# Decay products in PSUM halves, a new rank for the first layer, and a result stored in pieces of 64 tokens

## The chip, the cores and the metric
The program runs on one core of one Trainium2 chip. The metric is the device time of one execution in microseconds (us). Before the change it is 2306.92 us, the median of 3 runs (2304.29 to 2314.39).

## The reference, cut to what matters
Three layers follow one another. `B, H, S, D` = 4, 8, 768, 40.

```python
# 1. a recurrence over 768 steps for each of 32 heads, state is 40 x 40
for t in range(S):
    y[t] = r[t] @ state
    Sa = state @ a[t]
    state = state * w[t][None, :] - outer(Sa, b[t]) + outer(v[t], k[t])
# x: 3072 tokens x 320
# 2. first layer, d_ff = 2048, weights given as 64-bit floats
h = x @ w_in;  x = (h * cos(h)) @ w_out
# 3. second layer: 8 experts, d_ff = 1024
P = exp(logits - max); 8 rounds of dividing by row sums and column sums
out = sum over e of P[:, e] * (relu(x @ w1[e]) @ w2[e])
```

## The kernel before, in words
**Stages.** The recurrence is cut into 24 chunks of 32 steps. The 32 heads lie as 16 pairs, so that most attention tiles have 80 partitions (two heads of 40) and 16 blocks of 32 columns. For each chunk n there are three functions. `early(n)` (line 664) loads decays, a, b, k, r and v, forms the running products of the decays from the front and from behind, scales a, b and k with them, multiplies them on TensorE, and inverts a 32 x 32 triangle per head: the triangle goes through a DRAM tile (`LD`) into another layout, 62 small GpSimd instructions do the inversion (`inverse`, line 707), and the result goes back through another DRAM tile (`UD`). `late(n)` (line 722) fetches that inverse and prepares transposed factors. `chain(n)` (line 764) carries the state from chunk n-1 to chunk n and writes the chunk's output y to a DRAM tile `XT`. Chunks form pairs: after every second chunk `moe1(i)` (line 939) runs the first layer on the pair's 256 tokens and writes `ZD`. Only when the recurrence is over does its memory come free for the second layer (`moe2`, line 1068), a long run of matmuls on all 3072 tokens: for each expert, six groups of 512 tokens. `combine` (line 1037) adds an expert's part to an accumulator of 128 tokens x 320, and at the last expert stores it.

**Decays.** In `early` the decay tile P has 16 blocks of 33 columns (a marker column, then 32 decays) and one column behind them. Two scans over all 529 columns, on VectorE, multiply along; a constant tile `d1` restarts the product at every marker. The scan from behind writes another SBUF tile, Q. Then Q is divided by the block's full product (`iPC`), a is multiplied by the products from the front (80 x 1024), and b and k by the divided ones, in two halves of 80 x 512. Two ScalarE squares with a running sum fill `flag` and `flagP`, from which a number range is judged at the end of the recurrence. P is triple buffered: the load of chunk n+3 waits until chunk n's chain has read it.

**Order of the work.** No queue order is written by hand. A recorder takes all operations, and `order` (line 353) places them with a list scheduler that has its own costs. At each point an engine takes, of what is ready, the operation with the smallest key. The key is a rank from `PRIORITY` (line 577, the first number), and within a rank the longer way still to go comes first, with an offset in microseconds (base + slope x group number) that can push a group forward. A rank without a base goes by the order of the program. Before: the chain, the decoding of the first layer's weights (`prep`) and the first layer (`one`) have rank 0; `early`, `late` and `y` have rank 1. Where TensorE would idle during the scheduler's first 800 us, it places filler matmuls of 64 x 64 on a constant.

**PSUM.** The 8 banks form three pools: A (4 banks: attention, decoding, logits, the second layer's first product), M and N (2 each: the first layer's sums and products, and the second layer's sums). `nc.bank("A", False)` takes a bank at its first use, and it comes free after the last use.

**Decoding.** The 64-bit weights of the first layer come in 32 pieces. Each is decoded by five VectorE and several ScalarE instructions through a bank of pool A, beside the first chunks.

**The store.** At the last expert each of 24 accumulators (128 partitions x 320) goes out with one DMA on the SP queue, whose target is a view of 2 batches x 64 tokens x 320.

Of the kernel before, what the change touches and what calls it, by code (L numbers as in the profile page):

```python
# [6 lines left out]
F32 = mybir.dt.float32  # L7
F32R = mybir.dt.float32r
I32 = mybir.dt.int32
ALU = mybir.AluOpType  # L10
AF = mybir.ActivationFunctionType
AX = mybir.AxisListType
# [60 lines left out]
def lay_out(x):  # L73
# [17 lines left out]
    w = np.zeros((NCH, FR, U * (C + 1) + 1), rows["w"].dtype)  # L91
    w[:, :, :-1].reshape(NCH, FR, U, C + 1)[..., 1:] = rows["w"]
    out["tw"] = w
    out["tabk"] = np.concatenate([apart(rows["a"]), flat(rows["b"]), flat(rows["k"])], 2)
# [454 lines left out]
def sinkhorn(nc, ident, P, sk, red, ones, bank):  # L549
# [27 lines left out]
PRIORITY = {  # L577
    "chain": (0, 0, 0), "y": (1, 0, 0), "early": (1, 0, 0), "late": (1, 0, 0), "prep": (0, None, 0),
    "one": (0, 0, 0), "gate": (2, 0, 0), "two": (3, None, 0), "fetch": (4, None, 0),
}  # L580
# [11 lines left out]
class Kernel:  # L592
    def __init__(self, sb, ps, dr, a):
# [8 lines left out]
        self.at2 = tile("at2", AT2_COLS, F32)  # L602
        self.flag = tile("flag", NCH + 2, F32)
        self.nc = nc = Recorder(ps, {"A": (4, 5, 6, 7), "M": (0, 1), "N": (2, 3)}, {x.name for x in a.values()})
# [19 lines left out]
    def attention_setup(self):  # L624
# [3 lines left out]
        self.P = [t2(U * 33 + 1) for _ in range(3)]  # L628
        self.Q = t(U * 33 + 1)
        self.invP = self.Q[:, 1:].rearrange("p (u s) -> p u s", u=U)[:, :, 1:33]  # L630
        self.ABK = [t(4 * U * 32) for _ in range(3)]
# [19 lines left out]
        self.iPC = t2(U)  # L651
        self.flagP = t2(NCH)
        self.LD = [self.dr.tile([U, 2, C, C], F32, name=f"LD{i}") for i in range(2)]
# [10 lines left out]
    def early(self, n):  # L664
# [6 lines left out]
        self.load(n)  # L671
        nc.vector.tensor_tensor_scan(self.Q[0:80, ::-1], P[0:80, ::-1], c["d1"][0:80, ::-1], 0.0, op0=ALU.mult, op1=ALU.max)
        nc.vector.tensor_tensor_scan(P[0:80], P[0:80], c["d1"][0:80], 0.0, op0=ALU.mult, op1=ALU.max)
        nc.vector.reciprocal(self.iPC[0:80], P3[0:80, :, 32])
        nc.vector.tensor_tensor(self.invP[0:80], self.invP[0:80], self.iPC[0:80].unsqueeze(2).to_broadcast([80, U, 32]), op=ALU.mult)
        A2 = Ax[0:80].rearrange("p u (h s) -> p u h s", h=2)
        nc.vector.tensor_tensor(A2, A2, P3[0:80, :, 0:32].unsqueeze(2).to_broadcast([80, U, 2, 32]), op=ALU.mult)
        ps = nc.bank("A")
        for q in range(2):
            u = slice(8 * q, 8 * q + 8)  # L680
            nc.vector.tensor_tensor(BK[0:80, :, u], BK[0:80, :, u],
                                    self.invP[0:80, u].unsqueeze(1).to_broadcast([80, 2, 8, 32]), op=ALU.mult)
            for i in range(8 * q, 8 * q + 8):
                k, o = divmod(i, 2)
                nc.tensor.matmul(ps[64 * o:64 * o + 64, 64 * k:64 * k + 64], lhsT=Ax[0:80, i, :], rhs=BK[0:80, :, i, :],
                                 start=True, stop=True)
        g = ps.rearrange("p (u s) -> p u s", u=8)
        nc.scalar.activation(Lb, g[:, :, 0:32], AF.Copy)
        nc.vector.tensor_tensor(Lkm, g[:, :, 32:64], c["lmask"].unsqueeze(1).to_broadcast([128, 8, 32]), op=ALU.mult)
        ps = nc.bank("A")  # L690
        for x, f in ((P3[0:80, :, 1:33], self.flagP), (self.invP[0:80], self.flag)):
            nc.scalar.activation(ps[0:80].rearrange("p (u s) -> p u s", u=U), x, AF.Square, accum_out=f[0:80, n:n + 1])
        LD, UD = self.LD[n % 2], self.UD[n % 2]
# [158 lines left out]
    def moe1_weights(self):  # L852
# [20 lines left out]
        for f in range(16):  # L873
# [5 lines left out]
                out=s[:, 0:768].bitcast(I32), in_=a["win"].bitcast(I32)[f])  # L879
            A, Bl = decode(nc, self.c["expo"], st, nc.bank("A", False)[:, 0:384], w[:, 384:768].bitcast(F32R), -1)  # L880
            hi = w[:, 0:384].bitcast(F32R)
# [6 lines left out]
            nc.sync.dma_start(out=s[:, 0:640].bitcast(I32), in_=a["moe_w_out"].bitcast(I32)[128 * f:128 * f + 128, :])  # L888
            A, Bl = decode(nc, self.c["expo"], st, nc.bank("A", False)[:, 0:320], w[:, 960:1280].bitcast(F32R), -1)
            hi, lo = w[:, 640:960].bitcast(F32R), w[:, 960:1280].bitcast(F32R)  # L890
# [146 lines left out]
    def combine(self, e, t, ps4):  # L1037
        nc = self.nc
        out = self.a["out"]
        for j in range(4):  # L1040
# [9 lines left out]
            if e == E - 1:  # L1050
                i, j2 = divmod(tt, 2)
                nc.sync.dma_start(out=out.rearrange("(b t) d -> b t d", b=B)[2 * j2:2 * j2 + 2, 64 * i:64 * i + 64, :], in_=acc)

    def in_range(self):

        nc, f = self.nc, self.flag
        nc.group = ("gate", 0)
        nc.vector.tensor_reduce(f[0:80, NCH:NCH + 1], self.flagP[0:80], axis=AX.X, op=ALU.add)

    def decide(self, out):  # L1060
        nc, f = self.nc, self.flag
        nc.group = ("gate", 0)
        nc.vector.tensor_reduce(f[0:80, NCH + 1:NCH + 2], f[0:80, 0:NCH + 1], axis=AX.X, op=ALU.add)
        ps = nc.bank("A")
        nc.tensor.matmul(ps[0:1, 0:1], lhsT=f[0:80, NCH + 1:NCH + 2], rhs=self.ones[0:80, 0:1], start=True, stop=True)
        nc.vector.tensor_scalar(out[0:1, 0:1], ps[0:1, 0:1], 1e16, None, op0=ALU.is_lt)
# [243 lines left out]
```

## Time and profile before

| what | us |
|---|---|
| median of 3 runs | 2306.92 |
| the profiled execution | 2302.23 |
| its span, first to last instruction | 2300.5 |
| TensorE busy, 18773 matmuls | 2258.6 (98%) |
| VectorE busy | 1058.9 (46%) |
| ScalarE busy | 820.1 (36%) |
| GpSimd busy | 658.8 (29%) |
| mean granted TensorE clock | 0.995 |

Busy times are unions over the span. TensorE's counts the filler matmuls as well, so a busy TensorE is no proof of useful work in the first 800 us. All operations carry one line number (L519, the place where the scheduler's list is emitted), so that groups are told apart by their tiles and shapes: `at` are attention's tiles, `r1a` and `r1b` the weights (later the accumulators), `r` and `fs` the layers' working tiles, `cst` constants, `ps` PSUM.

### The profile page before, as it was taken

What the parts mean: (1) busy time and instruction counts of PE and PEld (TensorE: products, weight loads), DVE (VectorE), ACT (ScalarE), POOL (GpSimd) and SP (SyncE); (2) the same over time, 40 slices, a digit from 0 to 9 for tenths busy, and PEclk for the clock granted to TensorE, in tenths of its full rate; (3) what the DMA queues carried; (4) which work ended last, traced back from release to release, by engine and by line L of the source; (5) the groups of instructions that cost most, each with busy time, mean ns of one, the idle gap of its engine ahead of it and who ended that gap; (6) DMA issues with size and microseconds to landing.
All of it is one profiled execution on the core that took longest, in us unless ns stands there. A gap on an engine that the chain in (4) does not pass through costs nothing.

```text
span 2300.5 us, 45714 instructions
## 1 busy us (share of the span) xinstructions
PE 2258.6 (98%) x18773; PEld 2064.7 (90%) x18773; DVE 1058.9 (46%) x2106; ACT 820.1 (36%) x1710; POOL 658.8 (29%) x1694
## 2 busy tenths in 40 slices
PE   8999999999999999999999999999999999999997
PEld 7889999999999997999999989999988999999886
DVE  8878877888878653411222222222222222222222
ACT  5456655565656564224112112113113113112111
POOL 2858486677864731002002002002002002001000
PEclk9999999999999999999999999999999999999999
DMA  8343433444433233001001001001001001000000
GB/s 227 95 111 89 103 92 70 101 103 106 103 89 92 63 95 98 1 1 51 1 1 51 1 1 51 1 1 51 1 1 51 1 1 51 1 1 7 24 23 25
DMA packets 155496, 116.85 MB, mean 51 GB/s; under 512 B 112528, under 2 KB 134032, under 8 KB 153360
## 3 DMA queue, kind: packets, MB, share of 16 engines
q1 hardware_dynamic: 155280, 113.86, 19.7%
q8 instruction: 149, 2.44, 0.4%
q14 instruction: 67, 0.55, 0.1%
HBM read 95.73 MB, written 18.09 MB: 49 GB/s over the span
## 4 chain that ended last, share of the span: by engine, by line


## 5 line engine op out<-in xcount | busy, mean ns | idle before, releaser
L519 DVE SCALAR_TENSOR_TENSOR r<-ps,r 128x512 fp32r<-128x512 f32 x384 | 265.5, 692 | 971.0 <-ACT r L519 971.0
L519 PE MATMUL ps<-r1a,r 128*128 128x320 f32 x4248 | 669.5, 310 | 0.4 <-DVE r L519 0.4
L519 ACT ACTIVATE r<-ps 128x512 fp32r<-128x512 f32 x480 | 286.4, 597 | 1042.2 <-PE ps L519 1023.9
L519 PEld LDWEIGHTS ps<-r1a,r 128*128 128x128 f32 x4248 | 637.0, 188 | 15.5 <-DVE r L519 0.7
L519 POOL TENSOR_TENSOR at<-at 128x60 f32<-128x60 f32 (+24 forms) x1488 | 518.1, 348 | 276.0 <-DMA at<-LD 160.2
L519 PE MATMUL ps<-at,r1a 128*128 128x512 f32 x2352 | 579.1, 397 | 0.0
L519 PEld LDWEIGHTS ps<-at,r1a 128*128 128x128 f32 x2352 | 435.9, 188 | 93.8
L519 PE MATMUL ps<-at 128*64 128x72 f32 (+6 forms) x6064 | 446.4, 248 | 11.8 <-DMA at<-UD 4.6
L519 PEld LDWEIGHTS ps<-at 80*64 80x64 f32 (+4 forms) x6064 | 385.1, 147 | 54.7 <-issue 8.2
L519 POOL TENSOR_TENSOR r1a<-at,r1a 128x256 fp32r<-128x256 f32 (+2 forms) x147 | 101.4, 693 | 804.2 <-ACT r1a L519 794.5
L519 PE MATMUL ps<-at,r 128*128 128x320 f32 (+1 forms) x1128 | 182.6, 314 | 0.0
L519 PEld LDWEIGHTS ps<-at,r 128*128 128x128 f32 (+1 forms) x1128 | 167.4, 184 | 9.3
L519 PE MATMUL ps<-cst 128*64 128x64 f32 x2400 | 162.3, 225 | 4.3 <-DMA cst<-in_consts 4.1
L519 PEld LDWEIGHTS ps<-cst 128*64 128x64 f32 x2400 | 149.9, 139 | 14.0 <-issue 5.8
L519 PE MATMUL ps<-r,r1a 128*128 128x256 f32 x960 | 138.8, 291 | 3.1 <-ACT r L519 2.1
L519 POOL TENSOR_TENSOR at<-at,at 128x256 fp32r<-128x256 f32 (+2 forms) x45 | 31.1, 692 | 355.3 <-ACT at L519 350.2
L519 ACT ACTIVATE at<-ps 80x320 f32<-80x320 f32 (+4 forms) x234 | 92.7, 417 | 111.3 <-PE ps L519 98.4
L519 PEld LDWEIGHTS ps<-r,r1a 128*128 128x128 f32 x960 | 123.5, 193 | 6.6 <-ACT r L519 2.3
L519 DVE TENSOR_TENSOR at<-ps,at 80x256 f32<-80x256 f32 (+4 forms) x396 | 103.3, 317 | 19.3 <-ACT at L519 18.7
L519 DVE SCALAR_TENSOR_TENSOR r1b<-ps,fs,r1b 128x320 f32<-128x320 f32 x168 | 80.9, 544 | 36.9 <-PE ps L519 36.9
L519 ACT ACTIVATE fs<-ps,cst 128x512 int32<-128x512 f32 x96 | 65.7, 684 | 88.0 <-PE ps L519 78.6
L519 DVE SCALAR_TENSOR_TENSOR fs<-ps,fs 128x512 f32<-128x512 f32 x96 | 65.8, 685 | 57.3 <-ACT fs L519 56.9
(89 smaller groups left out, 1487.2 us busy)
## 6 DMA issues: line engine op xcount, KB each, us to landing
at<-in_w SPq DMA_DIRECT2D x64, 352.0 KB
at<-in_tabk SPq DMA_DIRECT2D x24, 640.0 KB
at<-LD SPq DMA_DIRECT2D x96, 128.0 KB
at<-in_trv SPq DMA_DIRECT2D x24, 480.0 KB
at<-in_tw SPq DMA_DIRECT2D x24, 165.3 KB
at<-in_nv SPq DMA_DIRECT2D x48, 80.0 KB
ZD<-fs SPq DMA_DIRECT2D x24, 160.0 KB
at<-ZD SPq DMA_DIRECT2D x24, 160.0 KB
```

What stands on the lines that cost most here:

```text
L519: getattr(getattr(nc, self.ENGINES[e]), method)(*[res(x) for x in args], **{n: res(x) for n, x in kwargs.items()})
```

## The change
- The decay scans are done in two halves of 8 blocks. ScalarE copies a half (80 x 264) into a PSUM bank; the scan from the front reads that copy and writes P; ScalarE copies the products from the front (8 x 31 columns) into the rest of the bank; the scan from behind then runs in place in the bank. The products from behind, their division by the block's product, and the factor for b and k are then read from PSUM. The tile Q is gone. The multiplication of a is done in two halves and leaves out the first column, whose factor is 1.
- The squares for the number range are four per chunk instead of two, written in place into the same banks; they get a group of their own with rank -1, ahead of all else.
- The first layer (`one`) goes from rank 0 to rank 1, with an offset of 260 us for the first pair that falls by 28 us with every pair.
- The decoding takes its banks from pool N instead of A.
- The result of each accumulator goes out in two DMAs of 64 tokens instead of one of 128.

```diff
     "chain": (0, 0, 0), "y": (1, 0, 0), "early": (1, 0, 0), ... "prep": (0, None, 0),
-    "one": (0, 0, 0), "gate": (2, 0, 0), ...
+    "range": (-1, 0, 0),
+    "one": (1, 260, -28), "gate": (2, 0, 0), ...
 def early(self, n):
-        nc.vector.tensor_tensor_scan(self.Q[0:80, ::-1], P[0:80, ::-1], c["d1"][0:80, ::-1], 0.0, ...)
-        nc.vector.tensor_tensor_scan(P[0:80], P[0:80], c["d1"][0:80], 0.0, ...)
+        half, inv, pre = U // 2 * (C + 1), [], []
+        for h in range(2):
+            at, to = slice(half * h + 1, half * h + half + 1), half * h + half
+            bank = nc.bank("A", False)[0:80]
+            w, d1 = bank[:, 0:half], c["d1"][0:80, at]
+            pre.append(bank[:, half:512].rearrange("p (u s) -> p u s", u=U // 2))
+            nc.scalar.activation(w, P[0:80, at], AF.Copy)
+            nc.vector.tensor_tensor_scan(P[0:80, half * h + 1:to], w[:, 0:half - 1], d1[:, 0:half - 1], 1.0, ...)
+            nc.scalar.activation(pre[h], P3[0:80, 8 * h:8 * h + 8, 1:32], AF.Copy)
+            nc.vector.tensor_tensor_scan(w[:, ::-1], w[:, ::-1], d1[:, ::-1], 1.0, ...)
+            inv.append(w.rearrange("p (u s) -> p u s", u=U // 2)[:, :, 1:C + 1])
         nc.vector.reciprocal(self.iPC[0:80], P3[0:80, :, 32])
-        nc.vector.tensor_tensor(self.invP[0:80], self.invP[0:80], iPC ...)          # 80 x 512
-        nc.vector.tensor_tensor(A2, A2, P3[0:80, :, 0:32] ...)                      # 80 x 1024
+        for h in range(2):
+            nc.vector.tensor_tensor(inv[h], inv[h], iPC ...)                        # 80 x 256
+            nc.vector.tensor_tensor(A2[:, u, :, 1:32], A2[:, u, :, 1:32], pre[h] ...)   # 80 x 496
             nc.vector.tensor_tensor(BK[0:80, :, u], BK[0:80, :, u],
-                                    self.invP[0:80, u] ...)
+                                    inv[q] ...)
-        ps = nc.bank("A")
-        for x, f in ((P3[0:80, :, 1:33], self.flagP), (self.invP[0:80], self.flag)):
-            nc.scalar.activation(ps[0:80] ..., x, AF.Square, accum_out=f[0:80, n:n + 1])
+        nc.group = ("range", n)
+        for h in range(2):
+            k = 2 * n + h
+            nc.scalar.activation(inv[h], inv[h], AF.Square, accum_out=self.flag[0:80, k:k + 1])
+            nc.scalar.activation(inv[h], P3[0:80, 8 * h:8 * h + 8, 1:33], AF.Square, accum_out=self.flagP[0:80, k:k + 1])
+        nc.group = ("early", n)
 moe1_weights:
-            A, Bl = decode(nc, self.c["expo"], st, nc.bank("A", False)[:, 0:384], ...)   # and 0:320
+            A, Bl = decode(nc, self.c["expo"], st, nc.bank("N", False)[:, 0:384], ...)
 combine, e == E - 1:
-                nc.sync.dma_start(out=out.rearrange("(b t) d -> b t d", b=B)[2 * j2:2 * j2 + 2, 64 * i:64 * i + 64, :], in_=acc)
+                for b in range(2):
+                    r = S * (2 * j2 + b) + 64 * i
+                    nc.sync.dma_start(out=out[r:r + 64], in_=acc[64 * b:64 * b + 64])
```

In the laid-out input the marker columns 0 and 264 of the decays become 1, and `flag` and `flagP` are twice as wide.

## Rows read from the trace of the kernel before

**Rows 1.** Stretches: busy us of PE, PEld, DVE, ACT, POOL; granted clock, DMA share, GB/s.

```profile
0.00:200.00 200.00, 191.34 (x2841) 172.17 (x2842) 162.09 (x363) 108.03 (x262) 114.75 (x320) 1.00 0.57 140
200.00:840.00 640.00, 624.28 (x7911) 598.61 (x7909) 502.97 (x1067) 378.38 (x845) 419.01 (x1194) 0.99 0.38 90
840.00:2284.50 1444.50, 1442.97 (x8025) 1293.94 (x8025) 393.79 (x678) 333.69 (x605) 125.04 (x181) 1.00 0.07 21
560.00:720.00 160.00, 155.70 (x2025) 148.57 (x2024) 137.08 (x285) 95.57 (x222) 109.39 (x297) 0.98 0.42 99
```

**Rows 2.** Groups with shapes, PE, 0 to 200 us: count, busy us, mean ns.

```profile
L519 PE MATMUL ps<-cst 128*64 128x64 f32 x1548 | 103.3, 226 | 4.3 <-DMA cst<-in_consts 4.1 <-issue 0.2
```

**Rows 3.** The same view, 200 to 840 us.

```profile
L519 PE MATMUL ps<-cst 128*64 128x64 f32 x852 | 59.0, 224 | 0.0
```

**Rows 4.** Waits of POOL, 40 to 840 us: total us, times, longest.

```profile
POOL at L519 <- DMA at<-LD: 160.2, 10, 41.3
```

**Rows 5.** Groups of the whole span: the inversion on POOL.

```profile
L519 POOL TENSOR_TENSOR at<-at 128x60 f32<-128x60 f32 (+24 forms) x1488 | 518.1, 348 | 276.0 <-DMA at<-LD 160.2
```

**Rows 6.** Stretches as in Rows 1: the inversions of chunks 11 and 4.

```profile
414.00:437.50 23.50, 23.20 (x276) 22.65 (x275) 16.86 (x39) 13.11 (x26) 18.50 (x63) 1.00 0.37 78
171.50:200.90 29.40, 27.73 (x427) 25.73 (x426) 22.98 (x50) 18.20 (x43) 24.41 (x63) 1.00 0.52 122
```

**Rows 7.** Timeline of POOL, 500.5 to 506 us: start, us, what, count.

```profile
500.56 5.89 POOL L519 TENSOR_TENSOR at<-at 128x52 f32<-128x52 f32 x7
```

**Rows 8.** Timeline of DVE, the same stretch.

```profile
501.77 1.21 DVE L519 TENSOR_TENSOR_SCAN at<-at,cst 80x529 f32<-80x529 f32 x1
503.24 1.21 DVE L519 TENSOR_TENSOR_SCAN at<-at,cst 80x529 f32<-80x529 f32 x1
```

**Rows 9.** Timeline of SP's queue: chunk 6's decay load and its triangle.

```profile
194.34 0.33 SPq L519 DMA_DIRECT2D at<-in_tw  x1
...
244.47 0.38 SPq L519 DMA_DIRECT2D LD<-at  x1
```

**Rows 10.** Timeline of DVE: chunk 6's last product before TensorE.

```profile
206.96 0.68 DVE L519 TENSOR_TENSOR at<-at 80x512 f32<-80x512 f32 x1
```

**Rows 11.** Groups with shapes, DVE, whole span.

```profile
L519 DVE TENSOR_TENSOR_SCAN at<-at,cst 80x529 f32<-80x529 f32 x48 | 60.3, 1257 | 6.3 <-DMA at<-in_tw 5.4
...
L519 DVE TENSOR_TENSOR at<-at 80x512 f32<-80x512 f32 x48 | 32.7, 707 | 0.0
...
L519 DVE TENSOR_TENSOR at<-at,at 80x1024 f32<-80x1024 f32 x24 | 27.9, 1162 | 0.0
...
L519 DVE TENSOR_TENSOR at<-ps,cst 128x256 f32<-128x256 f32 x24 | 10.0, 418 | 2.5 <-PE ps L519 1.7 <-ACT at L519 0.7
...
L519 DVE SCALAR_TENSOR_TENSOR fs<-ps,fs 128x512 f32<-128x512 f32 x96 | 65.8, 685 | 57.3 <-ACT fs L519 56.9
```

**Rows 12.** Groups with shapes, ACT, whole span.

```profile
L519 ACT ACTIVATE ps<-at 80x512 f32<-80x512 f32 x48 | 28.3, 590 | 4.2 <-DVE at L519 2.7 <-ACT at L519 0.7 <-DVE r L519 0.5
...
L519 ACT ACTIVATE at<-ps 80x256 f32<-80x256 f32 x46 | 17.5, 381 | 14.4 <-PE ps L519 14.2
...
L519 ACT ACTIVATION_READ_ACCUMULATOR ps<-at 80x1 f32 x48 | 9.2, 191 | 0.1
```

**Rows 13.** Timeline of DVE, chunk 13's decays beside chunk 11's chain.

```profile
442.04 1.27 DVE L519 TENSOR_TENSOR_SCAN at<-at,cst 80x529 f32<-80x529 f32 x1
...
448.81 0.95 DVE L519 SCALAR_TENSOR_TENSOR at<-ps,cst 64x288 f32<-64x288 f32 x2 [0.26 <-PE ps L519]
...
450.27 1.28 DVE L519 TENSOR_TENSOR at<-at 80x512 f32<-80x512 f32 x2
```

**Rows 14.** Timeline of SP's queue at the end.

```profile
2283.19 6.03 SPq L519 DMA_DIRECT2D out<-r1b  x4
```

**Rows 15.** Stretches as in Rows 1: behind the last combine; one `ZD` store.

```profile
2284.60:2298.90 14.30, 0.00 (x0) 0.00 (x0) 0.00 (x0) 0.00 (x0) 0.00 (x0) 0.66 0.14 49
869.50:871.10 1.60, 1.56 (x8) 0.79 (x7) 0.00 (x0) 0.35 (x2) 1.33 (x3) 1.00 0.88 195
```

**Rows 16.** Timeline of SP's queue: that `ZD` store and its reader.

```profile
869.51 0.32 SPq L519 DMA_DIRECT2D ZD<-fs  x1
871.09 0.95 SPq L519 DMA_DIRECT2D at<-ZD  x2
```

More of the change, by code (lines that the diff above doesn't have):

```diff
@@ L92, in lay_out @@
     w[:, :, :-1].reshape(NCH, FR, U, C + 1)[..., 1:] = rows["w"]
+    w[:, :, [0, U // 2 * (C + 1)]] = 1
     out["tw"] = w
@@ L577 @@
 PRIORITY = {
-    "chain": (0, 0, 0), "y": (1, 0, 0), "early": (1, 0, 0), "late": (1, 0, 0), "prep": (0, None, 0),
-    "one": (0, 0, 0), "gate": (2, 0, 0), "two": (3, None, 0), "fetch": (4, None, 0),
+    "chain": (0, 0, 0), "range": (-1, 0, 0), "y": (1, 0, 0), "early": (1, 0, 0), "late": (1, 0, 0), "prep": (0, None, 0),
+    "one": (1, 260, -28), "gate": (2, 0, 0), "two": (3, None, 0), "fetch": (4, None, 0),
 }
@@ L602, in __init__ @@
         self.at2 = tile("at2", AT2_COLS, F32)
-        self.flag = tile("flag", NCH + 2, F32)
+        self.flag = tile("flag", 2 * NCH + 2, F32)
         self.nc = nc = Recorder(ps, {"A": (4, 5, 6, 7), "M": (0, 1), "N": (2, 3)}, {x.name for x in a.values()})
@@ L628, in attention_setup @@
         self.P = [t2(U * 33 + 1) for _ in range(3)]
-        self.Q = t(U * 33 + 1)
-        self.invP = self.Q[:, 1:].rearrange("p (u s) -> p u s", u=U)[:, :, 1:33]
         self.ABK = [t(4 * U * 32) for _ in range(3)]
@@ L651, in attention_setup @@
         self.iPC = t2(U)
-        self.flagP = t2(NCH)
+        self.flagP = t2(2 * NCH)
         self.LD = [self.dr.tile([U, 2, C, C], F32, name=f"LD{i}") for i in range(2)]
@@ L671, in early @@
         self.load(n)
-        nc.vector.tensor_tensor_scan(self.Q[0:80, ::-1], P[0:80, ::-1], c["d1"][0:80, ::-1], 0.0, op0=ALU.mult, op1=ALU.max)
-        nc.vector.tensor_tensor_scan(P[0:80], P[0:80], c["d1"][0:80], 0.0, op0=ALU.mult, op1=ALU.max)
+        half, inv, pre = U // 2 * (C + 1), [], []
[5 more added lines that the diff above has]
+            nc.scalar.activation(w, P[0:80, at], AF.Copy)
+            nc.vector.tensor_tensor_scan(P[0:80, half * h + 1:to], w[:, 0:half - 1], d1[:, 0:half - 1], 1.0, op0=ALU.mult, op1=ALU.max)
+            nc.scalar.activation(pre[h], P3[0:80, 8 * h:8 * h + 8, 1:32], AF.Copy)
+            nc.vector.tensor_tensor_scan(w[:, ::-1], w[:, ::-1], d1[:, ::-1], 1.0, op0=ALU.mult, op1=ALU.max)
+            inv.append(w.rearrange("p (u s) -> p u s", u=U // 2)[:, :, 1:C + 1])
         nc.vector.reciprocal(self.iPC[0:80], P3[0:80, :, 32])
-        nc.vector.tensor_tensor(self.invP[0:80], self.invP[0:80], self.iPC[0:80].unsqueeze(2).to_broadcast([80, U, 32]), op=ALU.mult)
         A2 = Ax[0:80].rearrange("p u (h s) -> p u h s", h=2)
-        nc.vector.tensor_tensor(A2, A2, P3[0:80, :, 0:32].unsqueeze(2).to_broadcast([80, U, 2, 32]), op=ALU.mult)
+        for h in range(2):
+            u = slice(8 * h, 8 * h + 8)
+            nc.vector.tensor_tensor(inv[h], inv[h], self.iPC[0:80, u].unsqueeze(2).to_broadcast([80, 8, 32]), op=ALU.mult)
+            nc.vector.tensor_tensor(A2[:, u, :, 1:32], A2[:, u, :, 1:32], pre[h].unsqueeze(2).to_broadcast([80, 8, 2, 31]), op=ALU.mult)
         ps = nc.bank("A")
@@ L681, in early @@
             nc.vector.tensor_tensor(BK[0:80, :, u], BK[0:80, :, u],
-                                    self.invP[0:80, u].unsqueeze(1).to_broadcast([80, 2, 8, 32]), op=ALU.mult)
+                                    inv[q].unsqueeze(1).to_broadcast([80, 2, 8, 32]), op=ALU.mult)
             for i in range(8 * q, 8 * q + 8):
@@ L879, in moe1_weights @@
                 out=s[:, 0:768].bitcast(I32), in_=a["win"].bitcast(I32)[f])
-            A, Bl = decode(nc, self.c["expo"], st, nc.bank("A", False)[:, 0:384], w[:, 384:768].bitcast(F32R), -1)
+            A, Bl = decode(nc, self.c["expo"], st, nc.bank("N", False)[:, 0:384], w[:, 384:768].bitcast(F32R), -1)
             hi = w[:, 0:384].bitcast(F32R)
@@ L888, in moe1_weights @@
             nc.sync.dma_start(out=s[:, 0:640].bitcast(I32), in_=a["moe_w_out"].bitcast(I32)[128 * f:128 * f + 128, :])
-            A, Bl = decode(nc, self.c["expo"], st, nc.bank("A", False)[:, 0:320], w[:, 960:1280].bitcast(F32R), -1)
+            A, Bl = decode(nc, self.c["expo"], st, nc.bank("N", False)[:, 0:320], w[:, 960:1280].bitcast(F32R), -1)
             hi, lo = w[:, 640:960].bitcast(F32R), w[:, 960:1280].bitcast(F32R)
@@ L1057, in in_range @@
         nc.group = ("gate", 0)
-        nc.vector.tensor_reduce(f[0:80, NCH:NCH + 1], self.flagP[0:80], axis=AX.X, op=ALU.add)
+        nc.vector.tensor_reduce(f[0:80, 2 * NCH:2 * NCH + 1], self.flagP[0:80], axis=AX.X, op=ALU.add)
     def decide(self, out):
@@ L1062, in decide @@
         nc.group = ("gate", 0)
-        nc.vector.tensor_reduce(f[0:80, NCH + 1:NCH + 2], f[0:80, 0:NCH + 1], axis=AX.X, op=ALU.add)
+        nc.vector.tensor_reduce(f[0:80, 2 * NCH + 1:2 * NCH + 2], f[0:80, 0:2 * NCH + 1], axis=AX.X, op=ALU.add)
         ps = nc.bank("A")
-        nc.tensor.matmul(ps[0:1, 0:1], lhsT=f[0:80, NCH + 1:NCH + 2], rhs=self.ones[0:80, 0:1], start=True, stop=True)
+        nc.tensor.matmul(ps[0:1, 0:1], lhsT=f[0:80, 2 * NCH + 1:2 * NCH + 2], rhs=self.ones[0:80, 0:1], start=True, stop=True)
         nc.vector.tensor_scalar(out[0:1, 0:1], ps[0:1, 0:1], 1e16, None, op0=ALU.is_lt)
```

1 line of the change is left out of this document (removed).

## The prediction
> **What bounds the kernel now.** I read the busy shares by stretch first, then what TensorE does in them, then who waits for whom on GpSimd, then the end.
>
> From 840 us to the last combine TensorE is busy for 1443.0 of 1444.5 us [rows 1]: the second layer is bound by matmuls which the change doesn't touch. What can move lies ahead of 840 us and behind 2284.5 us.
>
> Ahead of 840 us TensorE looks as busy, but part of that is filler: 1548 matmuls and 103.3 us before 200 us [rows 2], 852 and 59.0 us behind [rows 3]. From 200 to 840 us the engine is idle for 640.0 - 624.3 = 15.7 us [rows 1]. Filler and idle time together, 74.7 us, are all that this stretch can give back; TensorE's own work in it is 565 us. VectorE is busy for 503.0 of 640 us, 79%, and for 137.1 of 160 us, 86%, in its fullest stretch [rows 1]. So no engine is a hard bound there: TensorE's gaps come from a chain of waits.
>
> The links of that chain: a chunk's decays, its triangle to DRAM, 62 GpSimd instructions, the inverse through DRAM, the state's step, and three chunks later the decay tile is free again. GpSimd's part is the longest. Its 1488 inversion instructions take 518.1 us, 21.6 a chunk [rows 5]. Two things lengthen it. First, it is held up by VectorE. In chunk 11's inversion, beside few decay products, the instructions are busy for 18.5 of 23.5 us; in chunk 4's for 24.4 of 29.4 us [rows 6]. A close look shows why: while VectorE runs two scans with both inputs in SBUF, of 1.21 us each [rows 8], seven GpSimd instructions take 5.89 us [rows 7], where seven of the 62 in 23.5 us would take 2.65. The difference, 3.2 us, is the two scans and a little more. Over 24 chunks the loss is 24 x (21.6 - 18.5) = 74 us of GpSimd's time. Second, it waits 160.2 us in ten places for the triangle's way through DRAM [rows 4], 41.3 of them before the first chunk. Chunk 6 shows how: its decays are fetched at 194.3 us and its last product is done at 206.96 + 0.68 = 207.6 us [rows 10], yet the triangle leaves only at 244.5 us [rows 9]. Between lie only 32 small matmuls and a copy, but these have rank 1, and the first layer, with rank 0, always has matmuls ready.
>
> **The change, part by part.** All sums are against the profiled execution, 2302.2 us (span 2300.5), which is 4.7 us under the median of the runs shown.
>
> *VectorE in the early part, per chunk.* Two rows give the price of an instruction with a PSUM operand: 512 columns take 0.685 us and 256 take 0.418 [rows 11], so 0.151 us and 1.04 ns a column; a scan of 529 columns takes 1.257 us, so with the same fixed part 2.09 ns a column. Removed: two scans (2.51), the division (0.71 by the row of the same shape), the product for a (1.16), two for b and k (1.41), together 5.80 us. Added: four scans of 264 columns or one less, 0.70 each (2.81), two divisions of 256 (0.84), two products of 496 columns (0.67 each, 1.34), two of 512 (1.37), together 6.35 us. That is +0.56 us a chunk, 13 us in all. The trace shows no scan from PSUM. From below, half of 1.257 us each would make the four scans no dearer than the two, and the sum +0.26 us a chunk. From above, a scan might cost its full 1.257 us at half the columns: +2.2 us a chunk more, 53 us in all. I take 0.70, since the row at hand has the same columns in all, and keep both ends. VectorE's share covers it: (503 + 12) / 640 is 80%.
>
> [...]
>
> *ScalarE, per chunk.* Four copies of 248 or 264 columns, 0.38 each by the 256-column row (0.59 by the 512-column row from above), 1.5 us. The squares go from 2 x (0.59 + 0.19) = 1.56 us to 4 x (0.38 + 0.19) = 2.28 [rows 12]. Together +2.2 us a chunk, about 47 us on 378.4 us of 640 [rows 1]: 59% becomes 66%. ScalarE has room, but the early part now goes back and forth between two engines: copy, scan, copy, scan. I put 2 us more on its latency. The three-deep decay buffer hides it where a chunk has slack, and it costs up to 24 x 2 = 48 us if it nowhere does.
>
> *GpSimd.* None of the scans and large products has two SBUF inputs any more, so I take away the 74 us of being held up. What is left is 18.5 us of instructions and 5 us between them, 23.5 us a chunk for 26.6.
>
> *The first layer's rank.* It now competes with the early and late parts by the way still to go. Chunk 6's matmuls would no longer wait 37 us behind it. Of the 160.2 us of waits I expect a third to go. TensorE's amount of work is unchanged, so the first layer is late only by what the early parts take from it, 32 small matmuls a chunk.
>
> *Decoding in pool N.* The first layer doesn't use N yet, so pool A gains room before 200 us. The decoding has 2 banks for 4, and each piece holds one for five VectorE instructions. VectorE, busy for 162 of 200 us [rows 1], sets its pace, so I count nothing; from both sides, 10 us won or lost.
>
> *How much of that reaches the end.* GpSimd gains 74 us and loses waits, but TensorE and VectorE then move up. If VectorE reaches the share of its fullest stretch, 86%, the stretch lasts (503 + 12) / 0.857 = 601 us instead of 640: -39. TensorE would then do its 565 us in 601, 94%. The floor is -74.7, where every filler goes; the other end is 0. I take -35, a little short of VectorE's figure for the added latency.
>
> *The store.* Behind the last combine every engine is still, and 14.3 us pass with a DMA share of 0.14 [rows 15], which is 2.2 of 16 DMA engines: four stores of 160 KB, issued in 6.03 us [rows 14], trickle out at 49 GB/s. A store of the same size whose outermost extent is 128 rows runs at a share of 0.88 [rows 15] and is read 871.09 - 869.51 = 1.6 us after its issue [rows 16]. With 64 rows outermost I take that speed. Eight issues from 2283.2 us on at 0.42 to 0.61 us put the eighth at 2286.1 to 2287.5, and landed 1.6 us later: 2287.7 to 2289.1 instead of 2298.9. That is -10.5 us; 0 if the pieces still run on two engines, -11.2 at best.
>
> Sum: 2302.2 - 35 - 10.5 = 2256.7 profiled, and 4.7 more for the runs: 2261 us.
>
> **The rivals.**
> 1. *Only the store counts.* GpSimd's freed time turns into waiting, since TensorE and VectorE are near full anyway: 2302.2 - 10.5 + 4.7 = 2296 us. For it: TensorE 97.5% busy from 200 to 840 us. Against: 59 us of that is filler.
> 2. *The whole slack goes.* Filler and idle time behind 200 us vanish: 2306.9 - 74.7 - 10.5 = 2222 us. Against it: VectorE would need 515 / 565 = 91%.
> 3. *Banks make it slower.* Two of pool A's four banks are held from a chunk's first copy to its last square. Before, first scan to last product ran from 442.0 to 451.5 us [rows 13]; copies and squares make 12 us of it. Chunk 11's chain began inside, at 448.8 us, and lives on the same pool. If a chain waits a third of the hold, 4 us, 24 of them cost 96 us: 2261 + 96 = 2357. It decides from 45.5 / 24 = 1.9 us a chunk. Against it: the decays are fetched when the chain three chunks before has just ended, so that most of the hold falls before the next chain.
> 4. *The pieces don't spread.* The stage gains as forecast and the store nothing: 2272 us.
>
> **How the numbers follow.** The forecast has 0.54, with its own range from 2240 to 2285 (stage gain 11 to 57 us); rival 1 has 0.14, rival 2 0.16, rival 3 0.11, rival 4 0.05. Within 0.5%, 11.5 us, no change can be told, so faster means under 2295.4. Forecast, rivals 2 and 4 are faster, and about a seventh of rival 1: 0.77. The same: 0.12. Slower: 0.11. The range reaches from rival 2 to just beyond rival 1: 2222 to 2303 us.
>
> **What would show it.** Right: inversions of 23 to 24 us in every chunk; fillers behind 200 us well under 852; last store landed within 5 us of the last combine; the second layer's full stretch starting some 35 us earlier. Wrong: inversions short but as many fillers (rival 1), none (rival 2), chains longer than before and waiting on a bank (rival 3), a DMA share near 0.14 at the end (rival 4). VectorE's early part at over 8 us a chunk would mean that PSUM scans are mispriced.

## The result and the profile after

The changed kernel takes 2248.95 us (median, 2246.41 to 2251.95) against 2310.02 us of the kernel before, timed beside it: a ratio of 0.9738 [0.971, 0.9765]. A second timing of the same kernel, beside a later round of experiments, gave 0.9749 [0.9732, 0.9766]. The forecast was 2261 us.

The profiled execution took 2251.95 us, 50.3 less than the one before. The two places that the prediction parted stand like this:

| | before, us | after, us | difference |
|---|---|---|---|
| last combine ends | 2284.5 | 2239.3 | -45.2 |
| from there to the end of the span | 15.9 | 10.8 | -5.1 |
| TensorE busy | 2258.6 | 2208.9 | -49.7 |
| of it fillers | 162.3 (2400) | 99.6 (1474) | -62.7 |
| last instruction of the recurrence's last chain | 823.2 | 746.8 | -76.4 |
| last store of the first layer's result to `ZD` issued | 869.8 | 828.2 | -41.6 |

TensorE's time accounts for all of the first line: 62.7 us of fillers went, its own work became 13.0 us longer (2096.3 to 2109.3 us), and its idle time ahead of the last combine grew by 4.5 us; together -45.2.

The stretches of the changed kernel, with the columns of [rows 1]:

```profile
0.00:200.00 200.00, 188.69 (x2758) 168.61 (x2758) 169.24 (x406) 126.54 (x334) 110.98 (x356) 1.00 0.58 148
200.00:840.00 640.00, 622.71 (x7366) 593.71 (x7366) 511.39 (x1156) 419.44 (x1022) 369.44 (x1185) 0.97 0.41 97
306.60:320.20 13.60, 12.93 (x152) 11.99 (x149) 9.84 (x22) 5.40 (x16) 10.86 (x36) 0.50 0.60 137
```

The fillers, first up to 200 us and then from 200 to 840 us (count, busy us, mean ns):

```profile
L520 PE MATMUL ps<-cst 128*64 128x64 f32 x1352 | 90.8, 227 | 4.2 <-DMA cst<-in_consts 4.2
L520 PE MATMUL ps<-cst 128*64 128x64 f32 x122 | 8.8, 225 | 0.0
```

Against [rows 2, 3] little changed in the first 200 us (1548 to 1352), but behind them 730 of 852 fillers are gone. TensorE is as busy as before, 622.7 of 640 us, and nearly all of that is now its own work. The granted clock says what it lost: 0.97 instead of 0.99, with stretches like the third line at 0.50, the lower of the two levels that these two traces record (1.00 and 0.50). Over all of the time ahead of the second layer there are 34.1 us at that level, 13.7 before. At half speed that would be up to (34.1 - 13.7) / 2 = 10 us of TensorE's longer work; this is an estimate. In the third line's stretch the first layer's matmuls of 128 x 256 take 454 ns each, where their mean over the whole span is 292.

GpSimd's inversion in the whole span, and its wait for the triangle from 40 to 840 us (total, times, longest), answer to [rows 5] and [rows 4]:

```profile
L520 POOL TENSOR_TENSOR at<-at 128x60 f32<-128x60 f32 (+24 forms) x1488 | 445.3, 299 | 272.9 <-DMA at<-LD 140.3
```

```profile
POOL at L520 <- DMA at<-LD: 140.3, 11, 37.9
```

The instructions lost 72.8 us, 518.1 to 445.3; the waits only 20 us. The row of waits is not a steady measure: a wait for several things is put down to the one that came last, and the row reads 110.0 us in the profile of the kernel before with the new store alone, which keeps the order of the instructions up to its end (shown with that run). All idle time ahead of the inversions is 276.0 us before [rows 5] and 272.9 here.

VectorE's new instructions, and then ScalarE's, as groups with shapes (count, busy us, mean ns):

```profile
L520 DVE TENSOR_TENSOR_SCAN ps<-ps,cst 80x264 f32<-80x264 f32 x48 | 32.8, 696 | 1.3 <-ACT ps L520 1.1
...
L520 DVE TENSOR_TENSOR_SCAN at<-ps,cst 80x263 f32<-80x263 f32 x48 | 32.0, 687 | 10.9 <-ACT ps L520 10.6
...
L520 DVE TENSOR_TENSOR at<-at,ps 80x512 f32<-80x512 f32 x48 | 31.1, 674 | 0.0
...
L520 DVE TENSOR_TENSOR at<-at,ps 80x496 f32<-80x496 f32 x48 | 30.6, 658 | 0.0
...
L520 DVE TENSOR_TENSOR ps<-ps,at 80x256 f32<-80x256 f32 x48 | 18.4, 416 | 0.0
```

```profile
L520 ACT ACTIVATE ps<-at 80x248 f32<-80x248 f32 x48 | 17.7, 372 | 8.2 <-DVE at L520 7.8
...
L520 ACT ACTIVATE ps<-at 80x264 f32<-80x264 f32 x48 | 17.6, 384 | 7.2 <-DMA at<-in_tw 7.0
...
L520 ACT ACTIVATE ps<-ps 80x256 f32<-80x256 f32 x48 | 17.2, 359 | 9.6 <-DVE at L520 9.4
```

Twice the means of VectorE's five groups make 6.26 us a chunk. The two engines do go back and forth, copy, scan, copy, scan. The end of each row, the idle time ahead of its instructions and what ended it, shows this as small waits: 10.6 us behind one scan's copy in the whole span.

Chunk 6's triangle left 50.1 us after its decays were fetched [rows 9]; in the changed kernel it takes 31.2 us, as SP's queue shows:

```profile
186.59 0.32 SPq L520 DMA_DIRECT2D at<-in_tw  x1
...
217.77 0.48 SPq L520 DMA_DIRECT2D LD<-at  x1
```

The end: VectorE's last combines, SP's stores (start, us, what, count), what SP waits for behind 2230 us, and two stretches.

```profile
2237.36 1.93 DVE L520 SCALAR_TENSOR_TENSOR r1b<-ps,fs,r1b 128x320 f32<-128x320 f32 x4 [0.88 <-PE ps L520]
```

```profile
2237.94 6.68 SPq L520 DMA_DIRECT2D out<-r1b  x8
```

```profile
SPq L1303 <- SPq L1303: 3.1, 1, 3.1
```

```profile
2239.30:2248.10 8.80, 0.00 (x0) 0.00 (x0) 0.00 (x0) 0.00 (x0) 0.00 (x0) 0.65 0.33 74
...
2246.00:2250.00 4.00, 0.00 (x0) 0.00 (x0) 0.00 (x0) 0.00 (x0) 0.00 (x0) 0.50 0.01 4
```

The DMA engines are done at 2246 us, and 4 us of the span follow with a share of 0.01. Line 1303 is the branch to the step-by-step recurrence, which SP takes behind its last store; it stands still there for 3.1 us. So the end is now set by SP: eight issues in 6.68 us, and then the branch.

### The profile page after: what moved, and what is told of

The parts are those of the page before. It is cut to its first block, busy times and chain, and to the rows that moved or that the text cites. A ratio compares the mean times of both kernels' runs of the same rounds, so it can differ in the third digit from the quotient of the medians.

```text
span 2250.1 us, 44278 instructions
## 1 busy us (share of the span) xinstructions
PE 2208.9 (98%) x17847; PEld 2016.5 (90%) x17847; DVE 1053.2 (47%) x2202; ACT 850.8 (38%) x1902; POOL 585.7 (26%) x1694
## 4 chain that ended last, share of the span: by engine, by line
## 5 line engine op out<-in xcount | busy, mean ns | idle before, releaser
L520 POOL TENSOR_TENSOR at<-at 128x60 f32<-128x60 f32 (+24 forms) x1488 | 445.3, 299 | 272.9 <-DMA at<-LD 140.3
L520 PE MATMUL ps<-at 128*64 128x72 f32 (+6 forms) x6064 | 454.7, 254 | 15.3 <-ACT at L520 6.0
L520 PEld LDWEIGHTS ps<-at 80*64 80x64 f32 (+4 forms) x6064 | 394.2, 152 | 60.9 <-ACT at L520 9.4
L520 DVE TENSOR_TENSOR at<-ps,at 80x64 f32<-80x64 f32 (+4 forms) x396 | 102.1, 316 | 16.1 <-ACT at L520 15.6
L520 PE MATMUL ps<-cst 128*64 128x64 f32 x1474 | 99.6, 226 | 4.2 <-DMA cst<-in_consts 4.2
L520 PEld LDWEIGHTS ps<-cst 128*64 128x64 f32 x1474 | 92.7, 141 | 10.9 <-issue 5.2
L520 PE MATMUL ps<-r,r1b 128*128 128x256 f32 x576 | 85.1, 292 | 2.5 <-DVE r L520 2.4
```

Source lines behind the costliest of these rows:

```text
L520: getattr(getattr(nc, self.ENGINES[e]), method)(*[res(x) for x in args], **{n: res(x) for n, x in kwargs.items()})
```

## Experiments

The first theory was that of the prediction: the halves free GpSimd, the rank shortens the waits, the two add up, the decoding's banks count nothing, the store adds its own. The rivals: one part alone makes it; the banks do; or the gain is GpSimd's freedom from VectorE alone.

### Four parts alone

Kernel before with the first layer's new rank:

```
-    "one": (0, 0, 0), "gate": (2, 0, 0), ...
+    "one": (1, 260, -28), "gate": (2, 0, 0), ...
```

> The kernel before with the first layer's new rank and offset alone. My theory (both parts are needed: GpSimd is the longest link while VectorE holds it up, and it also waits for triangles that stand behind the first layer): the waits of GpSimd on the triangles shrink to about half of 160 us, the inversions stay at 26 to 27 us each, so some 25 us are won: ratio to the kernel before 0.987 to 0.992. Rival 'rank alone' (the early parts' place behind the first layer was all of it): some 45 to 50 us, ratio 0.978 to 0.981. Rival 'halves alone': nothing, ratio 0.998 to 1.002.

Ratio 0.9985 [0.9973, 0.9997]. GpSimd's wait from 40 to 840 us, and its inversion:

```profile
POOL at L519 <- DMA at<-LD: 56.0, 6, 13.4
```

```profile
L519 POOL TENSOR_TENSOR at<-at 128x60 f32<-128x60 f32 (+24 forms) x1488 | 529.0, 356 | 239.4 <-DMA at<-LD 56.0 <-ACT ps L519 42.8 <-ACT r L519 23.1
```

The rank does what it should to this row of waits, 160.2 to 56.0 us, and the kernel is hardly faster. All idle time ahead of the inversions fell less, 276.0 to 239.4 us, as other waits took its place (42.8 and 23.1 us on ScalarE), and the inversions took 10.9 us more. The wait with the largest total was not the one that set the time.

Changed kernel with the old rank, the decoding in pool A and the old store, so that the halves alone are left:

```
-    "one": (1, 260, -28), ...
+    "one": (0, 0, 0), ...
-    nc.bank("N", False)[:, 0:384]      # and 0:320
+    nc.bank("A", False)[:, 0:384]
```

> The PSUM halves and the squares of their own group alone; the first layer keeps rank 0, the decoding pool A, the result its one store per 128 tokens. My theory: inversions of 23 to 24 us, but the early parts still stand behind the first layer, so GpSimd idles more: 15 to 25 us won, ratio 0.989 to 0.994. Rival 'halves alone': 45 us and more, ratio at or under 0.981. Rival 'rank alone': nothing or a little slower for the banks that are held, 0.998 to 1.005.

Ratio 1.0107 [1.0086, 1.0127]: slower than before, though the inversions are as short as in the changed kernel (446.7 us). TensorE's last decoding matmul, its fillers and GpSimd's wait:

```profile
254.50 0.71 PE L520 MATMUL ps<-r1b,nident 128*128 128x320 f32 x2
```

```profile
L520 PE MATMUL ps<-cst 128*64 128x64 f32 x3016 | 204.2, 226 | 3.9 <-DMA cst<-in_consts 3.9
```

```profile
POOL at L520 <- DMA at<-LD: 190.7, 13, 42.0
```

The decoding ends on TensorE at 255 us; before it ended at 176, in the changed kernel at 153.8. The first layer's first cosine comes at 268 us instead of 192. TensorE, with nothing to do, runs 3016 fillers. With both misses the first theory fell: the parts don't add.

Changed kernel with the products from behind in SBUF instead of PSUM, the products from the front in one bank; the scheduler orders it anew:

```
+        self.Q = t(U * 33)
+        bank = nc.bank("A", False)[0:80]
         for h in range(2):
-            bank = nc.bank("A", False)[0:80]
-            w, d1 = bank[:, 0:half], c["d1"][0:80, at]
-            pre.append(bank[:, half:512]...)
+            w, d1 = self.Q[0:80, half * h:half * h + half], c["d1"][0:80, at]
+            pre.append(bank[:, 256 * h:256 * h + 248]...)
```

> The changed kernel with the halves of the decays copied into SBUF instead of PSUM; the products from the front stay in one PSUM bank. The number of instructions and their columns are the same, but the four scans, the division and the products for b and k have two SBUF inputs again; and one bank of pool A is held instead of two. My theory (what counts is that VectorE no longer holds up GpSimd): inversions of 26 to 27 us again and a time 15 to 30 us over the changed kernel, ratio to the kernel before 0.980 to 0.987. Rival (what counts is the split into halves, or the banks): the same time as the changed kernel or less, ratio 0.970 to 0.975, with inversions that are longer but off the path.

Ratio 1.0077 [1.0055, 1.0099]. The stretch with the columns of [rows 1], and the inversion:

```profile
200.00:840.00 640.00, 605.68 (x7416) 578.92 (x7415) 494.78 (x1126) 392.63 (x970) 389.09 (x1201) 0.93 0.39 91
```

```profile
L520 POOL TENSOR_TENSOR at<-at 128x60 f32<-128x60 f32 (+24 forms) x1488 | 479.7, 322 | 318.7 <-DMA at<-LD 126.5 <-DMA at<-UD 38.4 <-DMA fs<-XT 20.0
```

The hold-up is back (479.7 for 445.3 us), but 34 us on GpSimd alone don't account for the 72 us by which the last combine is later. Neither the theory nor its rival had a kernel slower than before. The run also has 99.0 us at the lower clock, against 34.1, which is up to 32 us by the estimate used above, and another order of the work. It mixes three things; a run with the order kept follows below.

Kernel before with the store in pieces:

```
-    nc.sync.dma_start(out=out.rearrange(...)[2 * j2:2 * j2 + 2, 64 * i:64 * i + 64, :], in_=acc)
+    for b in range(2):
+        r = S * (2 * j2 + b) + 64 * i
+        nc.sync.dma_start(out=out[r:r + 64], in_=acc[64 * b:64 * b + 64])
```

> The kernel before with the store in pieces of 64 tokens alone. By the trace of the changed kernel the end then lies 10.8 us behind the last combine instead of 15.9: 5 us won, ratio 0.998. By my forecast's arithmetic it would be 10.5 us, ratio 0.9955. All else as before: 2400 fillers, inversions of 26 us.

Ratio 0.9963 [0.9949, 0.9976], that is 8.5 us, from 5.5 to 11.8. VectorE's last combines and SP's stores:

```profile
2286.41 1.93 DVE L519 SCALAR_TENSOR_TENSOR r1b<-ps,fs,r1b 128x320 f32<-128x320 f32 x4 [0.88 <-PE ps L519]
```

```profile
2286.99 6.33 SPq L519 DMA_DIRECT2D out<-r1b  x8
```

The span ends at 2298.2 us, 9.9 us behind the last combine instead of 15.9. The trace shows 6.0 us of the 8.5; this part stands by itself. The same profile also shows how much GpSimd's wait for the triangle, from 40 to 840 us, differs between two executions of one order; all idle time ahead of the inversions is 284.5 us here and 276.0 before:

```profile
POOL at L519 <- DMA at<-LD: 110.0, 10, 40.8
```

### Which banks, which rank

After the halves alone the second theory was: the halves hold two of pool A's four banks, the decoding needs the same pool, and the first layer starts when the decoding is done. The new banks and the rank are what makes the halves pay.

Changed kernel with the decoding in pool A:

```
-    nc.bank("N", False)[:, 0:384]      # and 0:320
+    nc.bank("A", False)[:, 0:384]
```

> The changed kernel with the decoding back in pool A. The first three runs showed that neither the rank nor the halves alone win anything, and with the halves alone the first layer began at 268 us instead of 192. Second theory (three parts need each other: the halves free GpSimd, the rank lets the early parts use that, and the decoding must leave pool A because an early part now holds two of its four banks): the first layer begins late, 210 us or more, and most of the gain is lost, ratio to the kernel before 0.985 to 1.0. Rival (as in my forecast, the decoding's pool counts for nothing): ratio 0.972 to 0.978.

Ratio 0.9883 [0.9858, 0.9908], 31 to 33 us worse than the whole change. TensorE's last decoding matmul and the fillers:

```profile
250.52 0.71 PE L520 MATMUL ps<-r1b,nident 128*128 128x320 f32 x2
```

```profile
L520 PE MATMUL ps<-cst 128*64 128x64 f32 x2432 | 163.5, 225 | 3.9 <-DMA cst<-in_consts 3.9
```

The same row of the changed kernel shows the other side:

```profile
153.13 0.71 PE L520 MATMUL ps<-r1b,nident 128*128 128x320 f32 x2
```

VectorE's part of the decoding is done at 178 us here and at 109.6 there, and the last matmuls come 73 us behind it here and 44 there. The first layer's first cosine comes at 264 us for 177. The change moves only the bank of a piece's VectorE instructions to pool N; the matmuls that follow (`low`) take theirs from pool A in both kernels, so that here a piece takes banks of A twice. The loss is rather understated: ahead of the second layer this run has nothing at the lower clock, the changed kernel 34.1 and 41.0 us.

Changed kernel with the old rank:

```
-    "one": (1, 260, -28), ...
+    "one": (0, 0, 0), ...
```

> The changed kernel with the first layer at rank 0 again. Second theory: inversions of 23 us, the first layer begins as early as in the changed kernel, but the early parts' small matmuls stand behind it and GpSimd idles between: ratio 0.982 to 0.992. Rival (the loss with the halves alone came from the decoding only, the rank counts for nothing): 0.972 to 0.978.

Ratio 0.9838 [0.9813, 0.9863], 20 to 23 us worse than the whole. GpSimd's wait and the fillers:

```profile
POOL at L520 <- DMA at<-LD: 165.6, 10, 45.8
```

```profile
L520 PE MATMUL ps<-cst 128*64 128x64 f32 x2096 | 142.3, 226 | 4.2 <-DMA cst<-in_consts 4.2
```

The first layer starts as early (170.7 us), but the last chain ends at 794.4 us for 746.8. TensorE is short of work later: from 200 to 840 us it runs 746 fillers, where the changed kernel runs 122.

```profile
L520 PE MATMUL ps<-cst 128*64 128x64 f32 x746 | 52.1, 224 | 0.0
```

That the first layer, with rank 0, spends its work too soon would explain this; it is a reading of the order, and no run shows it apart.

Kernel before with the new rank and the decoding in pool N, without the halves and with the old store (the edits of the two runs above, put in):

> The kernel before with the rank and the decoding in pool N, without the halves and with the old store. Second theory: inversions stay at 26 to 27 us, and GpSimd keeps the pace: ratio 0.990 to 0.998. Rival (rank and decoding are the gain, the halves none): 0.975 to 0.983.

Ratio 0.9911 [0.9883, 0.9938]. GpSimd's inversion:

```profile
L519 POOL TENSOR_TENSOR at<-at 128x60 f32<-128x60 f32 (+24 forms) x1488 | 536.6, 361 | 230.7 <-DMA at<-LD 92.8 <-DMA UD<-at 19.8 <-ACT fs L519 2.7
```

So the halves are worth something, given the other two. And so are the new banks without the halves: 0.9985 with the rank alone, 0.9911 here, some 17 us. The last decoding matmul, here and then with the rank alone:

```profile
146.44 0.54 PE L519 MATMUL ps<-r1b,nident 128*128 128x320 f32 x2
```

```profile
177.75 0.71 PE L519 MATMUL ps<-r1b,nident 128*128 128x320 f32 x2
```

Pool A was short before the halves came into it. Taking 0.0037 for the store from the runs that have it, the ratios without the store are:

| | old rank | new rank |
|---|---|---|
| no halves, decoding in A | 1.000 | 0.9985 |
| no halves, decoding in N | not run | 0.9911 |
| halves, decoding in A | 1.0107 | 0.992 |
| halves, decoding in N | 0.9875 | 0.9775 to 0.9786 |

Taking any one of the three away from the whole costs 20 to 33 us. The rank alone brings 0.15%, and the halves alone make the kernel 1.1% slower. These ratios hold the clock as well: 0 us at the lower level with the decoding in A, 6.8 with the old rank, 37.5 without the halves, 34.1 and 41.0 in the whole.

### How much is GpSimd's hold-up

Changed kernel in which the products from behind lie in three SBUF buffers in turn, while the order of the instructions and the banks held are kept as they are. In this kernel the range test comes out false, so that the step-by-step recurrence runs behind the main part; only the main part is read.

```
+        self.Qs = [t(U * 33 // 2) for _ in range(3)]
-            w, d1 = bank[:, 0:half], c["d1"][0:80, at]
+            w = <self.Qs[(2 * n + h) % 3][0:80, 0:half], scheduled as the bank>
```

> The changed kernel, with every instruction of the main program in the same order on its engine and the same banks held, but the halves' copies lie in SBUF, so that the four scans, the two divisions and the products for b and k have two SBUF inputs. (The earlier run with SBUF halves also let the scheduler make another order.) Theory: GpSimd is held up again by about 5 us of such instructions a chunk at most, inversions grow from 23.3 to 25 to 27 us, and the time by 10 to 30 us: ratio 0.978 to 0.987. Rival (holding up GpSimd is off the path; what the halves bring is the scheduler's other order): ratio 0.972 to 0.976.

The whole took 11792.16 us (ratio 5.117) for the reason given. VectorE's last combines, and the inversion:

```profile
2247.38 1.93 DVE L520 SCALAR_TENSOR_TENSOR r1b<-ps,fs,r1b 128x320 f32<-128x320 f32 x4 [0.88 <-PE ps L520]
```

```profile
L520 POOL TENSOR_TENSOR at<-at 128x60 f32<-128x60 f32 (+24 forms) x1488 | 487.4, 328 | 243.1 <-DMA at<-LD 112.9 <-ACT fs L520 14.3
```

GpSimd gets 42.1 us back of work, 445.3 to 487.4, and the last combine ends at 2249.3 us, 10.0 later than in the changed kernel's first profile and 4.4 later than in its second (2244.9). The clock is no reason, with 37.5 us at the lower level in the main part. The hold-up itself is thus worth some 4 to 10 us with the order kept, as far as one profile of this kernel tells, less than the 10 to 30 expected. By subtraction most of the 29 to 31 us of the halves lies in the order that the scheduler makes for them; no run tries that order by itself. The kernel's text has a reason for another order: `order` keeps a VectorE instruction with two SBUF inputs and a GpSimd instruction that reads SBUF apart in its plan (its variable `port`), and with the halves in PSUM these pairs are gone.

### The end, the offset and the fillers

The changed kernel again, beside the three kernels that follow (no edit):

> The changed kernel once more, beside the next three on one chip: ratio to the kernel before 0.971 to 0.977.

Median 2252.9 us, ratio 0.9749 [0.9732, 0.9766], 41.0 us at the lower clock.

Changed kernel, with the second piece of the last four accumulators issued on ScalarE's queue:

```
-                    nc.sync.dma_start(out=out[r:r + 64], in_=acc[64 * b:64 * b + 64])
+                    q = nc.scalar if b and t == 5 else nc.sync
+                    q.dma_start(out=out[r:r + 64], in_=acc[64 * b:64 * b + 64])
```

> The changed kernel, in which for the last four accumulators of each second-of-two token group the second piece goes out on ScalarE's queue instead of SP's. In the changed kernel's trace the eight last stores take SP 6.7 us to issue, their data are out 1.2 us behind the last issue, and then SP's branch at the end takes 3.5 us from the last issue to the next instruction. Theory (the end follows SP's issuing, not the data): four issues less are about 2.4 us and their stalls 2 us, the end comes 3 to 5 us earlier, 6 to 8 us behind the last combine instead of 10.8. Rival (the data's way sets the end): no change, 10 to 11 us.

Ratio 0.9713 [0.9694, 0.9732]. VectorE's last combines; SP's and ScalarE's issues; the last stretch:

```profile
2234.72 1.93 DVE L520 SCALAR_TENSOR_TENSOR r1b<-ps,fs,r1b 128x320 f32<-128x320 f32 x4 [0.88 <-PE ps L520]
```

```profile
2235.29 3.50 SPq L520 DMA_DIRECT2D out<-r1b  x4
```

```profile
2235.30 3.34 ACTq L520 DMA_DIRECT2D out<-r1b  x4
```

```profile
2240.40:2244.40 4.00, 0.00 (x0) 0.00 (x0) 0.00 (x0) 0.00 (x0) 0.00 (x0) 0.52 0.02 6
```

The eight issues take 3.5 us instead of 6.7, and the span ends 7.8 us behind the last combine instead of 10.8. The DMA engines are idle for the last 4 us again: the bound is SP's issuing and its branch (a wait of 3.6 us here), not the bytes. The rest of the gain over the changed kernel isn't the store's: the last combine itself came at 2236.64 us for 2244.9, in the same order of instructions, with 20.5 us at the lower clock for 41.0.

Changed kernel with another offset of the first layer:

```
-    "one": (1, 260, -28), ...
+    "one": (1, 300, -28), ...
```

> The changed kernel with the first layer's offset at 300 us instead of 260 (the slope of 28 us a pair stays). Theory (the offset only has to put the first layer about level with the early parts): within 1% of the changed kernel, ratio to the kernel before 0.972 to 0.983, on either side. Rival (260 is a sharp optimum that the gain hangs on): over 0.983.

Ratio 0.9712 [0.9695, 0.9728]. The stretch from 200 to 800 us here, and then in the changed kernel run beside it:

```profile
200.00:800.00 600.00, 590.61 (x7382) 565.65 (x7381) 497.29 (x1131) 403.72 (x986) 351.50 (x1161) 0.99 0.42 97
```

```profile
200.00:800.00 600.00, 580.80 (x7081) 557.02 (x7082) 491.71 (x1121) 394.68 (x974) 353.88 (x1165) 0.97 0.41 95
```

The gain doesn't hang on 260. This kernel is a little faster than the changed one. It has another order, and it differs by the clock: 0.99 for 0.97 in the stretch, 6.8 us at the lower level for 41.0. That is not one execution's chance: the mean granted clock is 0.996 to 0.998 in all five of its runs and 0.989 to 0.992 in all nine of the changed kernel. A kernel with this offset and the split issue together wasn't run.

Changed kernel without fillers:

```
-FILL_END = 8e5
+FILL_END = 0
```

> The changed kernel without any filler matmul. The change took 926 of 2400 fillers away, and TensorE's clock was granted at half for 34 us of the first 840 us instead of 14, each half-speed us costing half a us of matmuls. Theory (fillers keep the clock up where TensorE has little to do, which is mainly before 170 us): with none, the clock is at half for most of the first 170 us and the time is 15 to 50 us longer, ratio 0.980 to 0.996. Rival (the early stretch waits for other engines anyway): the clock falls, but the time stays, ratio 0.972 to 0.978.

Ratio 0.9961 [0.9949, 0.9973], 48 us slower than the changed kernel run beside it. Two stretches:

```profile
100.00:200.00 100.00, 76.28 (x788) 66.78 (x787) 68.88 (x178) 46.54 (x136) 59.21 (x205) 0.57 0.39 88
200.00:840.00 640.00, 607.00 (x7113) 577.09 (x7114) 502.82 (x1139) 409.71 (x999) 350.80 (x1170) 0.94 0.39 91
```

The clock is at 0.57 between 100 and 200 us, where the changed kernel with its fillers has 1.00, and 228.7 us run at the lower level in all. Fillers are room that a better order can use, but while there was room here they kept the clock up (1.00 for 0.57). The 48 us are not the clock's alone, though: without fillers the scheduler makes another order, and the last decoding matmul comes at 259.5 us for 153.8.

```profile
258.32 1.20 PE L520 MATMUL ps<-r1b,nident 128*128 128x320 f32 x2
```

VectorE's part of the decoding is done at 120.9 us here, and its banks are in pool N. A late end of the decoding can thus have another cause than that pool, and this run doesn't show which.

## Why the prediction was right, and where not

*The sum.* Forecast for the profiled execution: -35 in the stage and -10.5 at the end, -45.5; measured -45.2 and -5.1, -50.3. The total was close; the stage gave more and the store less than stated. Both medians of the changed kernel, 2248.95 and 2252.9 us, stand in the forecast's own range. That the total came so close is in part luck: of what the -35 rested on, GpSimd's hold-up is worth 4 to 10 us with the order kept and the shorter waits by themselves next to nothing, while a term that was put at nothing, the decoding's banks, is worth 31 to 33 us.

*VectorE and ScalarE.* The prices were right. Ten instructions were priced at 6.35 us a chunk and take 6.26: the scan of a half 0.69 to 0.70 us for 0.70, 256 columns 0.416 for 0.418, 496 and 512 columns 0.658 and 0.674 for 0.67 and 0.685. A copy takes 0.37 to 0.38 us for 0.38 and a square 0.36 for 0.38. The 13 us more for VectorE don't show in its total, which fell from 1058.9 to 1053.2 us; why is open. A product with one operand in PSUM is no dearer here than one with both in SBUF: 80 x 512 takes 0.674 us, where [rows 11] has 0.707.

*GpSimd.* The size was right, 72.8 us for 74 and 23.3 us an inversion for 23.5. The runs agree with the cause given, VectorE's instructions with two SBUF inputs: the inversions are short in every kernel with the halves in PSUM (23.2 to 23.4 us) and long in the two with these products in SBUF (24.8 and 25.1). But its worth was put too high. I argued that the gain comes from GpSimd's shorter part of the chain; with the order kept, that part brings 4 to 10 us.

*The waits.* The size and the meaning were wrong. A third of 160.2 us was to go; 20 us went, less than the 50 us by which this row differs between two profiles of one order (160.2 and 110.0). The run with the rank alone lost two thirds of the row and gained 0.15%.

*The step that failed: "so I count nothing; from both sides, 10 us won or lost".* The decoding's banks are worth 31 to 33 us of the whole. I took VectorE as what paces the decoding and didn't ask who else takes banks of pool A. In the changed kernel with the decoding in pool A the last decoding matmul comes at 251 us instead of 154, and the first layer, whose weights these are, starts 87 us later. That is the third rival's mechanism, two of four banks held by the halves, in a place where it wasn't looked for: not the chains but the start. The kernel without the halves gained some 17 us from the same banks, so the decoding was short of them even before.

*VectorE's share as the limit.* "If VectorE reaches the share of its fullest stretch" gave -39, cut to -35. In the changed kernel VectorE is busy for 82% of the time from 200 to 800 us (491.71 of 600 us in its second profile). What filled up was TensorE: its fillers behind 200 us fell from 59.0 to 8.8 us. The second rival, all slack gone, named the right bound. For the profiled execution it would mean 2302.2 - 74.7 - 10.5 = 2217 us, 35 less than measured. Those 35 us are 13.0 of longer work of TensorE, 17.3 of idle time and 8.8 of fillers still in that stretch, 5.4 that the store gave less, and 3.0 more of idle time elsewhere, less 12.5 us of fillers that went before 200 us.

*The store.* A mis-sized term. The pieces do spread, as forecast: the stretch behind the last combine has a DMA share of 0.33 for 0.14. Of 16 engines 0.14 is 2.2 and 0.33 is 5.3, more than two; that all 16 take part no row here shows. But eight issues took 6.68 us, not the 2.9 to 4.3 that 0.42 to 0.61 us apiece gave; four issues in 6.03 us [rows 14] had shown longer ones. The data were done at 2246 us, 6.7 us behind the last combine, where "within 5 us" was to show the forecast right. And SP's branch, 3.1 us, comes behind the last issue. The prediction followed the data to the end and not the queue that issues them.

*The rivals.* That only the store counts is refuted (0.9963 against 0.9738), and so is that the pieces don't spread. That the banks make it slower came true of the halves alone (1.0107).

What stays open: what holds the last decoding matmuls in pool A, instruction by instruction, and without fillers; which part of the new order brings most of what the halves are worth; the decoding in N without the other parts; and why one program spends 34.1 us at the lower clock in one execution and 41.0 in the next.

## What to carry to other kernels

When a schedule is made by a planner, parts of a change are not terms of a sum: scratch held longer in a pool, other users of that pool and the ranks decide together, so for each pool list who else takes from it and what starts when they are done. Judge waits by what the bound engine does meanwhile (here by the fillers), not by the total of one row, which here differed by 50 us between two executions of one order. Follow a store's end along the queue that issues it and past its last instruction, not along the bytes alone.

## What the hardware showed that I had not expected

The granted clock has a share in the smaller differences here. Without any filler 228.7 us ran at the lower level. Among the kernels with fillers their number doesn't decide: two profiles of one order with 2400 fillers had 13.7 and 23.9 us there, others 23.9 with 3016, 0 with 2432, 99.0 with 1984, 37.5 with 1900 and 6.8 with 1676, and the changed kernel 34.1 and 41.0 with 1474. In the changed kernel's first profile TensorE had waited before each of the four falls: in the 5 us ahead of them it was busy for 2.3 to 3.4 us. The lower level then held while it worked, as in the stretch at 306.6 us, in which it is busy for 12.93 of 13.60 us at 0.50, mostly with attention's matmuls of 32 and 72 columns (108 of 152).

Two edits that hardly change the amount of work, the offset and the queue of four stores, had 6.8 and 20.5 us there. Against 41.0 that is up to 17 and 10 us less lost, by the estimate at half speed, and their medians are 9.6 and 8.4 us ahead. The offset makes another order and has the better clock in every run; the queue of the stores keeps the order. Why either has it is open.

GpSimd's freedom showed little at the end: 42.1 us more work on an engine that is busy for a quarter of the time moved the last combine by 4 to 10 us.
